# Where a Trainium2 kernel keeps and asks for its weights between a dense stage and a 64-step loop

## The chip, the core and the metric

The kernel runs on one core of one Trainium2 chip. The metric is the device time of one execution in microseconds (us), as the median of several runs. The core has five engines that work side by side: TensorE (PE) multiplies matrices, VectorE (DVE) and ScalarE (ACT) work on elements, GpSimd (POOL) does so too, and SyncE (SP) issues transfers. Transfers (DMA) can be issued from SP, ACT and POOL; each of the three has a queue of its own, which the profile calls q1 (SP), q10 (ACT) and q0 (POOL).

## The reference

Two independent parts are computed and laid side by side in the output.

```python
# part A: a gated long convolution over 2048 rows, 1024 columns
kv = shifted(k, shift_k) * v
y  = irfft(rfft(kv padded) * rfft(ssm_k padded)) + kv * ssm_D
a  = q * y

# part B: attention with a memory, segment after segment (32 rows each, 64 segments)
mem = mem0                                    # 8 rows
for s in range(64):
    h = concat([mem, x[32 rows of s]])        # 40 rows x 1024
    q, k, v = h @ Wq, h @ Wk, h @ Wv          # 32 heads of 128
    o = softmax(mask(q k^T * scale)) v
    o = o @ Wo
    mem = o[:8]                               # goes into the next segment
    out[s] = o[8:]
```

Wq, Wk, Wv and Wo have 1024 x 4096 bf16 values each, 8.4 MB, 33.6 MB together[...].

## The kernel before, in words

**Weights.** Each of the four matrices is cut into 16 chunks of 128 partitions x 2048 values, 512 KB (0.524 MB) each. A chunk is named (m, kc, g): m is 0 for K, 1 for Q, 2 for V, 3 for the output weights; kc is its block of rows; g is the first or second half of the heads. `order` lists the 64 chunks in the order in which a segment uses them. The 21 that `STREAM` picks are *streamed*: they are copied once to a tensor WS in device memory and from there loaded into a ring of six slots (`wring`, line 658, on SP's queue) in every segment. Two of them are kept on the chip from the second segment on, so the loop has 1218 ring loads. The other 43 are *resident*: they lie on the chip during the whole loop.

**Homes of the residents.** `parts[0]` (12 chunks of K and Q, tiles `Wmid`) are loaded before the dense stage. `parts[1]` (19 chunks, tiles `Wres`) are the 11 resident chunks of V and 8 more called `extra`: four of K first half and four of Q second half. The last 12, `late` (two of Q, ten of the output weights, tiles `Wlate`), are loaded once everything before the loop is over.

**Stages.** Part A comes first: stage 1 (0 to some 125 us), the spectra (to some 300 us) and the last stage (to some 358 us). Into the gaps of A's spectra and last stage, `fill()` puts *dense* slices: for 8 rows of each segment, K and Q of all heads are computed ahead (`dense`, line 550), one call for each of K first half, K second half, Q first half, Q second half. Each call ends with one store of 2 MB, `REC<-stage` (line 562), on SP's queue; it consists of 8192 pieces of 256 bytes. Chunks that have no home yet go through `pw`, a rotating pool of eight tiles that is closed with the pre-loop scope. `group` (line 515) issues the loads of the eight chunks of one (m, g), and for streamed ones the copy to WS on POOL's queue (line 526).

After A, V of the same rows is computed (line 598): 2 halves x 4 row blocks x 4 column blocks x 8 chunks, 256 matmuls; their results go to VBD in 32 stores (line 602). The weights of the second half are asked for with the second half's `group` call. After V's calls `extra` is loaded (line 609), then `late` (line 614, in turn on SP and ACT), then the loop begins: six `fetch` calls fill the ring (line 658), the records of the first segment are loaded (`rec`, line 707), and the memory rows (Y0, line 725, on ACT's queue); the first transposes on PE (line 713) need Y0 and make the memory part of hT, which every projection needs.

**What sets the order.** Outside the loop a scheduler orders the instructions of each engine; so V loads, VBD stores and loads of `extra` stand interleaved on SP. The loop is ordered by hand (`tc.manual_schedule()`). An engine issues its instructions in order, its DMAs too. The DMAs of SP and ACT share eight completion semaphores in rotation; before one is used again, its issuer waits until the DMA that had it last has landed. A tile that takes the place of an earlier one waits until the earlier one's readers are done.

Of the kernel before, what the change touches and what calls it, by code (L numbers as in the profile page):

```python
# [9 lines left out]
BF = mybir.dt.bfloat16  # L10
# [15 lines left out]
N2, N3 = 12, 19  # L26
# [358 lines left out]
def b_kernel(ctx: ExitStack, tc, x, mem0, Wq, Wk, Wv, Wo, outb, n_seg, run_a):  # L385
    nc = tc.nc
    SEG = 32
    NX = 24
# [18 lines left out]
    streamed = set()  # L407
    for i in STREAM:
        streamed.add(order[i])
    resident = [ch for ch in order if ch not in streamed]  # L410
    groups = [(m, g) for m in (0, 1, 2) for g in range(2)]
    own = {mg: [ch for ch in resident if ch[0] < 3 and (ch[0], ch[2]) == mg] for mg in groups}
    parts = [(own[0, 1] + own[1, 0])[:N2], own[2, 0] + own[2, 1]]
    extra = [ch for ch in own[0, 0] + own[1, 1] + resident if ch not in parts[0] + parts[1]][:N3 - len(parts[1])]
    parts[1] = parts[1] + list(dict.fromkeys(extra))
    late = [ch for ch in resident if ch not in parts[0] and ch not in parts[1]]


    ring_order = [ch for ch in order if ch in streamed]
# [1 line left out]
    def dram_chunk(ch):  # L421
        m, a, g = ch
        return Wo_v[a] if m == 3 else W_v[m][a, g]

    def dst_view(ap, ch):
        return ap.rearrange("p (hh d) -> p hh d", hh=2) if ch[0] == 3 else ap

    def stream_src(ch):
        return WS[ring_order.index(ch), :, 0:2048]
# [3 lines left out]
    REC = dram.tile([128, n_seg, 768], BF, name="REC")  # L433
    VBD = dram.tile([n_seg, 8, 4, 4, 256], BF, name="VBD")
    WS = dram.tile([len(ring_order), 128, PITCH], BF, name="WS")
    res = {}
# [10 lines left out]

    c0 = ExitStack()
    xtp = c0.enter_context(tc.tile_pool(name="b0_xt", bufs=1, side="right"))
    pring = c0.enter_context(tc.tile_pool(name="b0_ring", bufs=8, side="right"))  # L450
    st = c0.enter_context(tc.tile_pool(name="b0_st", bufs=2, side="right"))
    XBT = xtp.tile([128, 8, n_seg, 8], BF, name="XBT")

    def pw():
        return pring.tile([128, 2048], BF, tag="pw", name="pw")

    def slot16(shape, dt, name):
        return st.tile(shape, dt, tag="stage", name=name)
# [4 lines left out]
    def stage1_done():  # L463
        make_consts()
        pools["mid"] = ctx.enter_context(tc.tile_pool(name="b_wmid", bufs=1, reuse_waits="tile"))
        for i, ch in enumerate(parts[0]):
            res[ch] = pools["mid"].tile([128, 2048], BF, name=f"Wmid{i}")[:]
        make_xbt()
        for _ in dense(0, 0):
            pass  # L470
# [41 lines left out]
            nc.scalar.copy(XBT[:, :, 16 * tb:16 * tb + 16, :].rearrange("p k s t -> p k (s t)"),  # L512
                           tp[:].rearrange("p (k c) -> p k c", k=8))

    def group(m, g):
        ws = []
        for kc in range(8):
            ch = (m, kc, g)
            if ch in res:
                nc.sync.dma_start(res[ch], dram_chunk(ch))  # L520
                ws.append(res[ch])
            else:
                t = pw()
                nc.sync.dma_start(t[:], dram_chunk(ch))
                if ch in streamed:
                    nc.gpsimd.dma_start(stream_src(ch), t[:])
                ws.append(t[:])
        return ws

    def x_block(b):  # L530
        X_sb = st.tile([128, 1024], BF, tag="X_sb", name="X_sb")
        xq[b % 2].dma_start(X_sb[:], x[b * 128:(b + 1) * 128, :])
        tp = ps0.tile([128, 1024], BF, tag="ps0", name="xt_ps")
        for kc in range(8):
            nc.tensor.transpose(tp[:, kc * 128:(kc + 1) * 128], X_sb[:, kc * 128:(kc + 1) * 128], ident[:])
        xt = st.tile([128, 4, 8, SEG], BF, tag="xt", name="xt")
        nc.vector.tensor_copy(xt[:], tp[:].rearrange("p (k j t) -> p j k t", k=8, j=4))
        nc.gpsimd.dma_start(REC[:, 4 * b:4 * b + 4, 0:256], xt[:].rearrange("p s k t -> p s (k t)"))
# [3 lines left out]
    def evac(dst, src):  # L542
        flip[0] ^= 1
        if flip[0]:
            nc.scalar.copy(dst, src)
        else:
            nc.vector.tensor_copy(dst, src)


    def dense(m, g, ws=None):  # L550
        ws = ws or group(m, g)
        stage = st.tile([128, n_seg, 16, 8], BF, tag="stage", name="stage")
        for hl in range(16):
            ps = ps0.tile([128, 512], F32, tag="ps0", name="kb_ps")
            for kc in range(8):
                nc.tensor.matmul(ps[:], lhsT=ws[kc][:, hl * 128:(hl + 1) * 128],  # L556
                                 rhs=XBT[:, kc].rearrange("p s t -> p (s t)"),
                                 start=(kc == 0), stop=(kc == 7))
            evac(stage[:, :, hl, :], ps[:].rearrange("p (s t) -> p s t", t=8))
            yield  # L560
        o = 256 * (m + 1) + 128 * g
        nc.sync.dma_start(REC[:, :, o:o + 128], stage[:].rearrange("p s h t -> p s (h t)"))

    def slices():
        k1, q0 = group(0, 1), group(1, 0)
        n = 0
        for m, g, ws in ((0, 1, k1), (1, 0, q0), (1, 1, None)):
            for _ in dense(m, g, ws):
                n += 1
                if n % 3 == 0:  # L570
                    x_block(n // 3 - 1)
                yield

    rest = slices()

    def fill():
        next(rest, None)

    run_a(pw, slot16, stage1_done, fill)

    wres3 = ctx.enter_context(tc.tile_pool(name="b_wres", bufs=1, reuse_waits="tile"))
    for i, ch in enumerate(parts[1]):
        res[ch] = wres3.tile([128, 2048], BF, name=f"Wres{i}")[:]

    with c0, c0p:
        for _ in rest:
            pass
        for ch in ring_order:
            if ch[0] == 3:
                nc.gpsimd.dma_start(dst_view(stream_src(ch), ch), dram_chunk(ch))  # L590
        for g in range(2):
            ws = group(2, g)
            for tb in range(4):
                vst = st.tile([128, 4, 512], BF, tag="stage", name="vst")
                for c in range(4):
                    ps = ps0.tile([128, 512], F32, tag="ps0", name="vb_ps")
                    for kc in range(8):
                        nc.tensor.matmul(ps[:], lhsT=XBT[:, kc, 16 * tb:16 * tb + 16, :].rearrange("p s t -> p (s t)"),
                                         rhs=ws[kc][:, c * 512:(c + 1) * 512], start=(kc == 0), stop=(kc == 7))
                    evac(vst[:, c, :], ps[:])  # L600
                for c in range(4):
                    nc.sync.dma_start(
                        VBD[16 * tb:16 * tb + 16, :, c, :, g * 128:(g + 1) * 128].rearrange("s t i e -> (s t) i e"),
                        vst[:, c, :].rearrange("p (i e) -> p i e", i=4))


        for ch in parts[1]:
            if ch in extra:
                nc.sync.dma_start(dst_view(res[ch], ch), dram_chunk(ch))

    wl = ctx.enter_context(tc.tile_pool(name="b_wlate", bufs=1, side="right", reuse_waits="tile"))
    for i, ch in enumerate(late):
        res[ch] = wl.tile([128, 2048], BF, name=f"Wlate{i}")[:]
        (nc.sync if i % 2 == 0 else nc.scalar).dma_start(dst_view(res[ch], ch), dram_chunk(ch))
    ring = ctx.enter_context(tc.tile_pool(name="b_ring", bufs=1, side="right", reuse_waits="tile"))
    one = ctx.enter_context(tc.tile_pool(name="b_one", bufs=1, side="right", reuse_waits="tile"))
    two = ctx.enter_context(tc.tile_pool(name="b_two", bufs=2, side="right", reuse_waits="tile"))
# [100 lines left out]
    with tc.manual_schedule():  # L718
# [3 lines left out]
        Y0 = one.tile([128, 256], BF, tag="PT", name="Y0")  # L722
        nc.vector.memset(Y0[:], 0.0)
        for dq in range(4):
            nc.scalar.dma_start(Y0[32 * dq + NX:32 * dq + SEG, :], mem0[:, dq * 256:(dq + 1) * 256])
        nc.tensor.matmul(SB[:], lhsT=ident[:], rhs=QBm[:].rearrange("p c i w -> p (c i w)"), start=True, stop=True,
                         skip_group_check=True)

# [43 lines left out]
        for s in range(n_seg):  # L772
# [132 lines left out]
            q0 = Proj(1, 0).run(4)  # L905
# [3 lines left out]
            q0 = q0.run(4).evac()  # L909
            k1 = Proj(0, 1).run(4)  # L910
            QT0 = one.tile([128, 4, 4, 32], BF, tag="QT", name="QT")
            nc.vector.tensor_copy(QT0[:], transposes(q0))
            k1 = k1.run(4).evac()
            scores(0, QT0, KT0)
            softmax_a()
            q1 = Proj(1, 1).run(4)
# [4 lines left out]
            q1 = q1.run(4).evac()  # L921
# [18 lines left out]
            if last:  # L940
                own = Tail(OTB, b, ps_acc.tile([128, 512], F32, tag="acc", name="own_acc")[:, 0:256])
# [21 lines left out]
def kernel(  # L963
# [26 lines left out]
    with ExitStack() as ctx_b:  # L990
        b_kernel(ctx_b, tc, B_x[0], B_mem0[0],
                 B_Wq.rearrange("d h e -> d (h e)"), B_Wk.rearrange("d h e -> d (h e)"),
                 B_Wv.rearrange("d h e -> d (h e)"), B_Wo.rearrange("h e d -> (h e) d"),
                 outb, n_seg, run_a)
# [35 lines left out]
```

## Time and profile before

| what | value |
|---|---|
| median of 7 runs | 2194.92 us (2188.84 to 2202.79) |
| the profiled execution, its own time | 2193.48 us |
| its span in the profile | 2191.7 us |
| PE, DVE, ACT, POOL busy | 79%, 40%, 29%, 19% of the span |
| moved by DMA | 807.80 MB, mean 369 GB/s |
| first matmul of V, last matmul of V | 379.1 us, 442.9 us |
| first matmul of the loop's first projection | 464.6 us |

The page divides the span into 40 slices of 54.8 us; a digit is the busy share of a slice in tenths. A line of waits names the waiting engine and line, what it waited for, the total in us, how often, and the longest. A line of an engine's order in time has start and length in us; "SPq", "ACTq" are the DMA instructions of those engines' queues, and their length is what the issue took, not the transfer. In "us to landing" a DMA is counted from issue until its data are there.

### The profile page before, as it was taken

How to read it: one execution, taken by the hardware profiler on the slowest of the kernel's cores; microseconds unless marked ns; L12 is line 12 of the kernel's file. 1: busy time of each engine (PE TensorE's matmuls, PEld its weight loads, DVE VectorE, ACT ScalarE, POOL GpSimd, SP SyncE). 2: the span in 40 equal slices, each digit the busy share in tenths (PEclk: the TensorE clock that was granted, in tenths of full speed). 3: DMA queues.
4: the chain of work that ended last, by engine and by line, in shares of the span. 5: the costliest groups of instructions: out<-in, count | busy, mean ns of one | idle time of the engine just before them, and what ended most of it. 6: DMA issues, size and time to landing. Idle time of an engine off the chain costs nothing. (4 is left out here: it accounts for less than half of the span.)

```text
span 2191.7 us, 81529 instructions
## 1 busy us (share of the span) xinstructions
PE 1722.7 (79%) x35636; PEld 927.2 (42%) x35636; DVE 884.6 (40%) x2702; ACT 638.9 (29%) x1118; POOL 412.9 (19%) x1103
## 2 busy tenths in 40 slices
PE   4679975957888888888887888887878878887886
PEld 2233332424444444444444444444444444444444
DVE  8828853123333333333333333333333333333333
ACT  5845620112222222222222222222222222222222
POOL 5003421001111111111111111111111211111111
PEclk9889987979999999999999999999999999999999
DMA  9989989899999999999999999999999999999997
GB/s 322 349 294 364 306 259 319 256 358 398 383 375 391 381 375 388 394 372 392 394 393 378 394 394 393 391 395 389 392 393 377 394 392 383 390 391 382 387 394 272
DMA packets 294286, 807.80 MB, mean 369 GB/s; under 512 B 84940, under 2 KB 84972, under 8 KB 293927
## 3 DMA queue, kind: packets, MB, share of 16 engines
q1 hardware_dynamic: 263592, 738.36, 89.1%
q0 software_dynamic: 23536, 50.51, 6.9%
q10 hardware_dynamic: 6800, 13.72, 1.7%
q8 instruction: 279, 4.57, 0.9%
q14 instruction: 79, 0.65, 0.1%
HBM read 743.06 MB, written 62.39 MB: 368 GB/s over the span
## 5 line engine op out<-in xcount | busy, mean ns | idle before, releaser
L806 PEld LDWEIGHTS <-rec 128*32 128x32 bf16 x12351 | 324.1, 96 | 468.1 <-issue 248.7
L806 PE MATMUL acc<-wring,rec 128*32 128x512 bf16 (+1 forms) x3777 | 375.9, 386 | 132.6 <-DMA wring<-WS 116.9
L815 ACT CAST qkv_sb<-acc 128x512 bf16<-128x512 f32 x384 | 225.1, 586 | 674.0 <-PE acc L806 670.9
L806 PE MATMUL acc<-Wres,rec 128*32 128x512 bf16 x4864 | 394.4, 383 | 0.3 <-issue 0.3
L892 PEld LDWEIGHTS <-OT 128*32 128x32 bf16 x8192 | 216.8, 96 | 178.9 <-issue 152.5
L892 PE MATMUL yacc<-Wlate,OT 128*32 128x256 bf16 x5120 | 221.0, 273 | 14.8 <-issue 13.5
L892 PE MATMUL yacc<-wring,OT 128*32 128x256 bf16 x3072 | 154.6, 276 | 98.3 <-DMA wring<-WS 58.5
L806 PE MATMUL acc<-Wmid,rec 128*32 128x512 bf16 x3072 | 224.9, 382 | 0.0
L752 PEld LDWEIGHTS <-OTB 128*16 128x16 bf16 x4096 | 105.4, 90 | 104.4 <-issue 93.8
L878 ACT CAST OT<-OTp 128x512 bf16<-128x512 f32 x128 | 75.0, 586 | 242.2 <-PE OTp L870 239.1
L908 DVE COPY KT<-tps 128x512 bf16<-128x512 bf16 x64 | 27.2, 425 | 292.4 <-PE tps L821 292.4
L707 POOL DMA_DIRECT2D rec<-REC x64 | 37.4, 584 | 566.3 <-issue 269.8
L879 DVE CAST OTB<-OTp 128x128 bf16<-128x128 f32 x128 | 37.3, 292 | 262.6 <-ACT OT L878 262.6
L647 DVE TENSOR_SCALAR wring<-OTp 128x384 int32<-128x384 int32 x126 | 112.3, 891 | 55.9 <-PE acc L806 52.7
L752 PE MATMUL SB<-Wlate,OTB 128*16 128x256 bf16 x2480 | 100.9, 283 | 34.6 <-DVE SB L743 19.7
L782 POOL COPY KT<-rec 128x128 bf16<-128x128 bf16 x128 | 38.7, 302 | 436.0 <-PE SB L830 427.9
L836 DVE TENSOR_REDUCE mx<-SB 128x5 f32<-128x200 f32 x128 | 47.1, 368 | 179.5 <-PE SB L830 179.5
L767 POOL DMA_DIRECT2D out_dram<-YB x128 | 73.1, 577 | 238.8 <-DVE YB L765 215.5
L752 PE MATMUL SB<-wring,OTB 128*16 128x256 bf16 x1488 | 78.5, 273 | 37.0 <-DVE SB L731 29.8
L821 PE MATMUL tps<-ident,qkv_sb 128*128 128x128 bf16 x1024 | 101.0, 221 | 8.0 <-DVE wring L647 0.2
L821 PEld LDWEIGHTS <-qkv_sb 128*128 128x128 bf16 x1024 | 62.7, 97 | 104.9 <-ACT qkv_sb L815 67.1
L556 PE MATMUL kb_ps<-XBT,pw 128*128 128x512 bf16 x320 | 87.7, 397 | 9.9 <-ACT XBT L512 8.0
(214 smaller groups left out, 2304.8 us busy)
## 6 DMA issues: line engine op xcount, KB each, us to landing
wring<-WS SPq DMA_DIRECT2D x1218, 512.0 KB, 7.2
rec<-REC POOLq DMA_DIRECT2D x64, 192.0 KB, 5.9
SK<-s_sb SPq DMA_DIRECT2D x16, 512.0 KB, 4.4
SU<-s_sb SPq DMA_DIRECT2D x16, 512.0 KB, 4.3
Ug<-SU SPq DMA_DIRECT2D x32, 256.0 KB, 6.0
Kg<-SK ACTq DMA_DIRECT2D x32, 256.0 KB, 5.5
REC<-stage SPq DMA_DIRECT2D x4, 2048.0 KB, 15.4
SZ<-zs SPq DMA_DIRECT2D x31, 256.0 KB, 3.4
```

Of the source, the lines that this page charges most:

```text
L556: nc.tensor.matmul(ps[:], lhsT=ws[kc][:, hl * 128:(hl + 1) * 128], rhs=XBT[:, kc].rearrange("p s t -> p (s t)"), start=(kc == 0), stop=(kc ...
L647: nc.vector.tensor_scalar(out=dst, in0=src, scalar1=0, scalar2=None, op0=ALU.bitwise_or)
L707: nc.gpsimd.dma_start(rec[:], REC[:, s, :])
L752: nc.tensor.matmul(self.acc[32 * dq:32 * dq + W, x - o:y - o], lhsT=self.OTB[:, c, 4 * g + i, :], rhs=r, start=first and not self.seeded, ...
L767: nc.gpsimd.dma_start(bass.AP(outb.tensor, outb.offset + (SEG * NB * self.b + NX) * 2048 + 256 * dq, [[2048 * SEG, NB], [2048, 8], [1, 256 ...
L782: nc.gpsimd.tensor_copy(KT[:, :, :, 32:40], KBs[:, 128 * g:128 * g + 128].rearrange("p (c i t) -> p i c t", c=4, i=4))
L806: nc.tensor.matmul(self.acc[32 * c:32 * c + 32, x - 512 * c:y - 512 * c], lhsT=hT[:, kc, :], rhs=r, start=(kc == 0 and x == 512 * c), stop ...
L815: nc.scalar.copy(sb[:], self.acc[:])
L821: nc.tensor.transpose(tp[:, i * 128:(i + 1) * 128], sb[:, i * 128:(i + 1) * 128], ident[:])
L836: nc.vector.tensor_reduce(out=mx[:], in_=S, op=ALU.max, axis=AX.X)
L878: nc.scalar.copy(OT[:], o_view[:, :, :, 0:32])
L892: nc.tensor.matmul(yacc[32 * dq:32 * dq + 32, x - o:y - o], lhsT=OT[:, c, i, :], rhs=r, start=(h == 0 and x == o), stop=(h == 31), tile_po ...
```

## The change

It does five things. (1) Six of the eight Q second-half chunks, those that are resident (`kept_q1`), get the `pw` tiles in which the dense stage uses them as their home for the loop; `pw` becomes eight tiles with fixed tags in a pool that stays open, and the loads of the eight chunks are asked for at the start of Q first half (six) and of Q second half (two). `extra` then holds the four K chunks and four output chunks, and `late` six output chunks, of which two take the remaining `pw` tiles. (2) All 16 V loads are issued ahead of V's first matmul: the five streamed ones go into three tiles of later `extra` chunks and into two `pw` tiles. (3) `extra` is loaded on POOL's queue: five chunks ahead of V compute, three when V is done with their tiles. (4) `late` is issued on ACT's queue alone, so that the ring loads follow the VBD stores on SP directly; Y0 is loaded on POOL's queue. (5) The four REC stores move from SP's to ACT's queue.

```diff
--- before.py
+++ after.py
@@ -411,9 +411,11 @@
     groups = [(m, g) for m in (0, 1, 2) for g in range(2)]
     own = {mg: [ch for ch in resident if ch[0] < 3 and (ch[0], ch[2]) == mg] for mg in groups}
     parts = [(own[0, 1] + own[1, 0])[:N2], own[2, 0] + own[2, 1]]
-    extra = [ch for ch in own[0, 0] + own[1, 1] + resident if ch not in parts[0] + parts[1]][:N3 - len(parts[1])]
-    parts[1] = parts[1] + list(dict.fromkeys(extra))
-    late = [ch for ch in resident if ch not in parts[0] and ch not in parts[1]]
+    kept_q1 = own[1, 1][:6]
+    placed = parts[0] + parts[1] + kept_q1
+    extra = [ch for ch in own[0, 0] + own[1, 1] + resident if ch not in placed]
+    extra = list(dict.fromkeys(extra))[:N3 - len(parts[1])]
+    late = [ch for ch in resident if ch not in placed and ch not in extra]
 
 
     ring_order = [ch for ch in order if ch in streamed]
@@ -447,12 +449,17 @@
 
     c0 = ExitStack()
     xtp = c0.enter_context(tc.tile_pool(name="b0_xt", bufs=1, side="right"))
-    pring = c0.enter_context(tc.tile_pool(name="b0_ring", bufs=8, side="right"))
+    pring = ctx.enter_context(tc.tile_pool(name="b0_ring", bufs=1, reuse_waits="tile"))
     st = c0.enter_context(tc.tile_pool(name="b0_st", bufs=2, side="right"))
     XBT = xtp.tile([128, 8, n_seg, 8], BF, name="XBT")
 
-    def pw():
-        return pring.tile([128, 2048], BF, tag="pw", name="pw")
+    pw_next = [0]
+
+    def pw(k=None):
+        if k is None:
+            k = pw_next[0] % 8
+            pw_next[0] += 1
+        return pring.tile([128, 2048], BF, tag=f"pw{k}", name="pw")
 
     def slot16(shape, dt, name):
         return st.tile(shape, dt, tag="stage", name=name)
@@ -512,19 +519,19 @@
             nc.scalar.copy(XBT[:, :, 16 * tb:16 * tb + 16, :].rearrange("p k s t -> p k (s t)"),
                            tp[:].rearrange("p (k c) -> p k c", k=8))
 
-    def group(m, g):
-        ws = []
-        for kc in range(8):
+    def group(m, g, temps={}, which=range(8), ws=None):
+        ws = ws or [None] * 8
+        for kc in which:
             ch = (m, kc, g)
             if ch in res:
                 nc.sync.dma_start(res[ch], dram_chunk(ch))
-                ws.append(res[ch])
+                ws[kc] = res[ch]
             else:
-                t = pw()
+                t = temps[ch]() if ch in temps else pw()
                 nc.sync.dma_start(t[:], dram_chunk(ch))
                 if ch in streamed:
                     nc.gpsimd.dma_start(stream_src(ch), t[:])
-                ws.append(t[:])
+                ws[kc] = t[:]
         return ws
 
     def x_block(b):
@@ -559,12 +566,21 @@
             evac(stage[:, :, hl, :], ps[:].rearrange("p (s t) -> p s t", t=8))
             yield
         o = 256 * (m + 1) + 128 * g
-        nc.sync.dma_start(REC[:, :, o:o + 128], stage[:].rearrange("p s h t -> p s (h t)"))
+        nc.scalar.dma_start(REC[:, :, o:o + 128], stage[:].rearrange("p s h t -> p s (h t)"))
 
     def slices():
         k1, q0 = group(0, 1), group(1, 0)
+        q1 = [None] * 8
+        first = [kc for kc in range(8) if (1, kc, 1) in kept_q1]
+        rest = [kc for kc in range(8) if kc not in first]
         n = 0
-        for m, g, ws in ((0, 1, k1), (1, 0, q0), (1, 1, None)):
+        for m, g, ws in ((0, 1, k1), (1, 0, q0), (1, 1, q1)):
+            if (m, g) == (1, 0):
+                for ch, k in zip(kept_q1, (4, 5, 6, 7, 0, 1)):
+                    res[ch] = pw(k)[:]
+                group(1, 1, which=first, ws=q1)
+            if (m, g) == (1, 1):
+                group(1, 1, {(1, kc, 1): (lambda k=k: pw(k)) for kc, k in zip(rest, (2, 3))}, rest, q1)
             for _ in dense(m, g, ws):
                 n += 1
                 if n % 3 == 0:
@@ -580,7 +596,13 @@
 
     wres3 = ctx.enter_context(tc.tile_pool(name="b_wres", bufs=1, reuse_waits="tile"))
     for i, ch in enumerate(parts[1]):
-        res[ch] = wres3.tile([128, 2048], BF, name=f"Wres{i}")[:]
+        res[ch] = wres3.tile([128, 2048], BF, tag=f"Wres{i}", name="Wres")[:]
+
+    def more(i):
+        return wres3.tile([128, 2048], BF, tag=f"Wmore{i}", name="Wmore")
+
+    v_temp = [(2, kc, g) for g in range(2) for kc in range(8) if (2, kc, g) in streamed]
+    homes_v = [lambda i=i: more(i) for i in range(len(v_temp) - 2)] + [lambda k=k: pw(k) for k in (2, 3)]
 
     with c0, c0p:
         for _ in rest:
@@ -588,8 +610,14 @@
         for ch in ring_order:
             if ch[0] == 3:
                 nc.gpsimd.dma_start(dst_view(stream_src(ch), ch), dram_chunk(ch))
+        temps = dict(zip(v_temp, homes_v))
+        wv = [group(2, g, temps) for g in range(2)]
+        for i, ch in enumerate(extra):
+            if i >= len(v_temp) - 2:
+                res[ch] = more(i)[:]
+                nc.gpsimd.dma_start(dst_view(res[ch], ch), dram_chunk(ch))
         for g in range(2):
-            ws = group(2, g)
+            ws = wv[g]
             for tb in range(4):
                 vst = st.tile([128, 4, 512], BF, tag="stage", name="vst")
                 for c in range(4):
@@ -603,15 +631,16 @@
                         VBD[16 * tb:16 * tb + 16, :, c, :, g * 128:(g + 1) * 128].rearrange("s t i e -> (s t) i e"),
                         vst[:, c, :].rearrange("p (i e) -> p i e", i=4))
 
-
-        for ch in parts[1]:
-            if ch in extra:
-                nc.sync.dma_start(dst_view(res[ch], ch), dram_chunk(ch))
+        for i, ch in enumerate(extra):
+            if i < len(v_temp) - 2:
+                res[ch] = more(i)[:]
+                nc.gpsimd.dma_start(dst_view(res[ch], ch), dram_chunk(ch))
 
     wl = ctx.enter_context(tc.tile_pool(name="b_wlate", bufs=1, side="right", reuse_waits="tile"))
     for i, ch in enumerate(late):
-        res[ch] = wl.tile([128, 2048], BF, name=f"Wlate{i}")[:]
-        (nc.sync if i % 2 == 0 else nc.scalar).dma_start(dst_view(res[ch], ch), dram_chunk(ch))
+        t = pw(2 + i) if i < 2 else wl.tile([128, 2048], BF, name=f"Wlate{i}")
+        res[ch] = t[:]
+        nc.scalar.dma_start(dst_view(res[ch], ch), dram_chunk(ch))
     ring = ctx.enter_context(tc.tile_pool(name="b_ring", bufs=1, side="right", reuse_waits="tile"))
     one = ctx.enter_context(tc.tile_pool(name="b_one", bufs=1, side="right", reuse_waits="tile"))
     two = ctx.enter_context(tc.tile_pool(name="b_two", bufs=2, side="right", reuse_waits="tile"))
@@ -722,7 +751,7 @@
         Y0 = one.tile([128, 256], BF, tag="PT", name="Y0")
         nc.vector.memset(Y0[:], 0.0)
         for dq in range(4):
-            nc.scalar.dma_start(Y0[32 * dq + NX:32 * dq + SEG, :], mem0[:, dq * 256:(dq + 1) * 256])
+            nc.gpsimd.dma_start(Y0[32 * dq + NX:32 * dq + SEG, :], mem0[:, dq * 256:(dq + 1) * 256])
         nc.tensor.matmul(SB[:], lhsT=ident[:], rhs=QBm[:].rearrange("p c i w -> p (c i w)"), start=True, stop=True,
                          skip_group_check=True)
 
```

## The prediction

> **What bounds the kernel now.** I read three lines of the page first: the slices, the DMA queues and the DMA issues.
>
> ```profile
> PE   4679975957888888888887888887878878887886
> DMA  9989989899999999999999999999999999999997
> GB/s 322 349 294 364 306 259 319 256 358 398 383 375 391 381 375 388 394 372 392 394 393 378 394 394 393 391 395 389 392 393 377 394 392 383 390 391 382 387 394 272
> ...
> q1 hardware_dynamic: 263592, 738.36, 89.1%
> ...
> wring<-WS SPq DMA_DIRECT2D x1218, 512.0 KB, 7.2
> REC<-stage SPq DMA_DIRECT2D x4, 2048.0 KB, 15.4
> ```
>
> A slice is 54.8 us. From the ninth on the core moves 375 to 395 GB/s with its DMA engines over 90% busy, and q1, SP's queue, carries 738 of the 808 MB. That is the loop: 1218 ring loads of 512 KB, bound by transfers. In the first eight slices, 0 to about 460 us, the rate is 256 to 364 GB/s: there something other than bytes is late. The waits of PE between 300 and 520 us name it:
>
> ```profile
> PE vb_ps L598 <- DMA Wres<-in_B_Wv_dram: 24.5, 5, 20.2
> PE tps L713 <- DMA Y<-in_B_mem_dram: 13.2, 1, 13.2
> PE y_ps L375 <- DMA zt<-SZ: 10.2, 5, 4.7
> ```
>
> (Columns: total us, times, longest.) V's weights cost 24.5 us, one wait of 20.2; the memory rows Y hold the loop's first transposes for 13.2. Why were the weights late? SP's own queue in order of time (start, duration):
>
> ```profile
> 355.29 0.34 SPq L524 DMA_DIRECT2D pw<-in_B_Wv_dram  x1
> 356.33 0.33 SPq L381 DMA_DIRECT2D out_dram<-ot  x1
> 357.56 0.56 SPq L562 DMA_DIRECT2D REC<-stage  x1
> 359.37 10.77 SPq L381 DMA_DIRECT2D out_dram<-ot  x1
> ```
>
> The small output store behind the 2 MB REC store took 10.77 us to issue, so SP gets free 12.6 us after the REC store went out, and the next V load stands at 370.73. The same happens behind the stores at 160.97 (next DMA 13.59 us) and 225.60 (10.80 us). The three stages, read from the windows:
>
> ```profile
> 360.00:370.00 10.00, 0.00 (x0) 0.00 (x0) 0.47 (x1) 0.00 (x0) 0.56 (x1) 0.59 1.08 261
> ...
> 430.00:440.00 10.00, 10.00 (x48) 4.52 (x47) 1.68 (x3) 1.76 (x3) 0.00 (x0) 1.00 0.42 86
> 440.00:450.00 10.00, 3.06 (x15) 1.18 (x12) 1.81 (x5) 0.59 (x1) 0.00 (x0) 0.86 0.83 258
> 450.00:460.00 10.00, 0.61 (x1) 0.10 (x1) 0.77 (x4) 0.00 (x0) 1.99 (x7) 0.50 1.04 378
> ```
>
> After the stretch and its length the first column is PE's busy time, the last two are DMA share and GB/s. PE stands from 358.9 to 379.1; then it computes V without a break from 389.8 (last first-half weight at 388.7) to 442.9; then it stands again until 464.6, while the DMA engines load what is still missing.
>
> **What the Trainium skill says.** "DMA: Bandwidth & Descriptors", section "Issuing engines are not separate DMA queues": DMAs from several engines run on the same 16 DMA engines and interleave; another issuer only saves sequencer time. The trace agrees on the engines: while the REC store ran at 360 to 370 their share stood at 1.08 with only 261 GB/s moved. But the sequencer time here is 12 us, not small. The same page, "Queues, rings and completion order": each DMA engine takes turns between queue rows packet by packet. The trace fits: beside the REC store at 225.6, key gathers on ACT's queue took 6.7 us to land, against 5.5 over all. So a REC store on ACT's queue lets SP's loads pass, but each slows the other.
>
> **The change part by part.** Six of the eight Q second-half chunks stay where the dense stage put them; they were loaded again later (4 as Wres, 2 as Wlate). Removed: 6 x 0.524 = 3.15 MB, at the loop's 390 GB/s 8.1 us of DMA time. Where it lay decides its worth. The four Wres reloads went out between 406 and 426 under V compute, with PE full: nothing saved directly, but their places are refilled by four output chunks that stood in the late list. So the late list after V falls from 12 to 6 chunks, 3.15 MB, and that is on the path.
>
> *Spectra stage (140 to 300 us).* The REC stores move to ACT's queue. SP no longer stops for some 12 us twice; PE idled about 3 us in each of the stretches 180 to 200 and 240 to 260, and part of it may come back. Against this, the next key gather on ACT stands eight to ten operations behind each store. ACT runs these in 8 to 10 us (13 casts in 10.2 us at 225 to 235), the queue is free after 12.3, so ACT stops for 2 to 5 us twice, with spectrum casts queued behind and PE waiting for those. Four Q loads also go out earlier, beside the first store. Gain and loss cancel: I take 0, bounds -5 to +6.
>
> *Last stage of A (300 to 358).* The last SZ store issued at 296.20 took 3.96 us behind a REC store; the first zt load needs it. That goes; the second zt load now waits for the REC store to land, as it did before. I take -2, bounds -4 to +1.
>
> *V start.* In the built program's order all 16 V loads follow A's last output store (about 361 us). Two go out earlier, but they are second-half chunks. SP issues four first-half chunks by 364. The fifth, (2,4,0), then waits on the completion semaphore that it shares with the last REC store: eight such semaphores go round over the DMAs of SP and ACT. The REC store alone needs some 9.5 us of DMA time (2.1 MB at the 218 GB/s seen beside it); sharing with four V chunks, two early ones, copies to WS and POOL's output chunks it lands about 377 to 380 instead of 372. Then 2.5 us of issue and 7.5 to 8.2 of landing (the Wres row) give 387 to 390, less the 2 us of the part above; before, 388.7. So the 11 us stall is mostly replaced by another wait: I take -2, bounds -10 (REC lands early) to +5. V compute, 256 matmuls at 0.216 us = 55.3, is unchanged.
>
> *Between V and loop.* Late loads sit on ACT alone, the ring is first on SP, Y rows on POOL. The Y wait goes, and so does SP's queue of late loads ahead of the ring (first ring load 457.8, 15 us after V). Late next: the third ring load shares a semaphore with the first late load, which lands 9.3 us after issue, so it goes out about 11 us after V, lands at 18; before, its like landed at about 24. The byte count agrees. From 440 to the first Y at 492.6 the engines moved 19.2 MB; 3.15 less and 0.5 more (one extra chunk that waits for V's end) are 16.6 MB, at 390 GB/s 42.5 us after V instead of 49.7. I take -6, bounds -10 to -2.
>
> *Loop.* Instruction order is the same on PE, DVE, ACT and POOL, and the ring still carries 1218 loads: 0. That cover is the DMA rate itself. If residents moved in SBUF changed it, 1% would be 17 us; nothing in the trace suggests it.
>
> Sum: 0 - 2 - 2 - 6 = **-10 us**. The profiled execution took 2193.48 (span 2191.7); it becomes 2183.5. The median of the seven runs lies 1.4 above it, so I predict 2185 for the median.
>
> **Rivals.**
> 1. *REC out of the way (large gain).* If REC lands within 15 us even when shared, V's first half is complete about 377, 11 earlier; with 2, 8 from the tail and 3 from the spectra stage, -24: 2171. For it: gathers beside a REC store were slowed by only 1.2 us. Against: those were 256 KB pieces, here some 5 MB compete.
> 2. *Tail hidden anyway (no change).* If A's stage and V start lose what the tail wins, say +3, 0, +2 and -5, the result is 2195. For it: the fifth V load's semaphore, and the third ring load's.
> 3. *ACT pays for SP (slower).* The REC store on ACT blocks the casts in the spectra stage: Kg gathers come after the queue is free and are late for their set too, 6 us at each of the two stores, and REC lands after 385, so that V starts 6 later: +12 +6 - 6 = +12: 2207. It decides once ACT's stop behind a store is over about 6 us, that is, if it reaches the gather in under 6 us. For it: PE was over 95% busy in much of this stage, so a stop counts in full. Against: eight casts took 8 us and more.
>
> **How the numbers follow.** A measurement of this kernel can tell about 0.3%, 6.6 us, from no change. Likeliest case (2178 to 2191) 0.50, rival 1 0.22, rival 2 0.18, rival 3 0.10. Below 2188.3 lie 0.44 of the likeliest case and all of rival 1: faster 0.66. The other 0.06 of the likeliest case and 0.16 of rival 2 make same 0.22; slower 0.12 is rival 3 and the upper 0.02 of rival 2. The range, 2168 to 2198, leaves out rival 3 and the lower end of rival 1, some 0.08: about 2 in 10.
>
> **What would show it.** In the changed profile: SP issues without the 10 us store behind REC; ACT's DMA issues show a 2 to 5 us one behind REC at about 173 and 237; V's first-half loads come in two parcels, four near 361 and four after 377; V compute ends near 439; the wait of tps on Y is gone and the loop's first matmul comes about 10 us after V, followed by a ring wait. HBM reads fall by 3.1 MB. Wrong would be: V ending before 430 (rival 1) or after 446 (rival 3), or loop windows of 100 us whose rate differs from 391 GB/s by over 1%.

## The result, and the profile after

The changed kernel is slower: 2215.84 us, median of 14 runs (2207.10 to 2222.17), against 2196.80 for the kernel before beside it (35 runs). The ratio is 1.0079, interval 1.0062 to 1.0097. The forecast was 2185. The profiled execution took 2214.37 us, its span is 2212.4.

The page of the kernel after, the lines that answer to those shown of before:

```profile
PE   4677986667778887888788888887887877888886
DMA  9978879879999999999999999999999999999996
GB/s 324 354 285 290 273 250 342 268 239 388 389 381 383 389 388 390 392 388 386 391 394 391 395 387 395 391 390 387 396 391 372 393 377 377 390 390 391 391 391 268
...
q1 hardware_dynamic: 228104, 722.63, 85.5%
...
HBM read 739.92 MB, written 62.39 MB: 363 GB/s over the span
...
REC<-stage ACTq DMA_DIRECT2D x4, 2048.0 KB, 25.0
```

From the tenth slice on the rate is what it was, 372 to 396 GB/s but for the last slice (before: 372 to 398): the loop did not change. The loss lies in the first nine slices, which moved 239 to 354 GB/s; the fourth went from 364 to 290 and the ninth from 358 to 239. HBM read fell from 743.06 to 739.92 MB, the 3.1 MB that the kept Q chunks should save. Queue q1 carries 723 MB instead of 738. And a REC store now takes 25.0 us to land, as the page's median, where it took 15.4.

To place the loss I read five starts of matmuls from the trace and use them for every kernel below: the last of the spectra (z_ps), the last of A (y_ps), the first and last of V (vb_ps), and the first of the loop's first projection.

| us | spectra end | A end | V first to last | loop starts | V end - A end | loop start - V end | span - loop start |
|---|---|---|---|---|---|---|---|
| before | 295.2 | 358.6 | 379.1 to 442.7 | 464.6 | 84.1 | 21.9 | 1727.1 |
| after | 319.6 | 377.0 | 389.8 to 468.9 | 488.2 | 91.9 | 19.3 | 1724.2 |

So the spectra stage lost 24.4 us, of which A's last stage gave 6.0 back; V's stage lost 7.8; the step from V to the loop won 2.6, the loop 2.9. The sum is +20.7, the difference of the spans.

**Spectra.** ACT's own order in time, 155 to 260 us, in the kernel after (start, duration):

```profile
161.59 0.59 ACTq L569 DMA_DIRECT2D REC<-stage  x1
171.35 13.71 ACTq L276 DMA_DIRECT2D Kg<-SK  x1
...
239.29 0.54 ACTq L569 DMA_DIRECT2D REC<-stage  x1
249.46 5.47 ACTq L276 DMA_DIRECT2D Kg<-SK  x1
```

The first key gather behind each of these two REC stores took 13.71 and 5.47 us to issue. ACT's casts stood behind it; PE waits, 100 to 380 us:

```profile
PE Ure_ps L306 <- ACT Kre L318: 15.1, 2, 12.1
```

PE was busy for 39.7 us of the three stretches 160 to 180, 180 to 200 and 240 to 260 taken together; in the kernel before it was busy for 53.7 of the same 60. The first of the three, before and after (PE's busy time follows the length):

```profile
160.00:180.00 20.00, 19.58 (x118) 7.13 (x118) 17.27 (x30) 12.29 (x24) 7.60 (x8) 1.00 1.05 310
```

```profile
160.00:180.00 20.00, 12.73 (x73) 4.69 (x72) 11.02 (x18) 5.18 (x10) 6.37 (x8) 0.90 1.04 360
```

SP, which the move was meant to free, stood too. Its waits, 160 to 300 us, in the kernel after:

```profile
SPq L527 <- DMA REC<-stage: 17.9, 1, 17.9
```

Five Q loads went out between 160.2 and 168.7 us; the sixth waited until the store had landed and stands at 186.68. The two have no data in common; what ties them is a shared completion semaphore, the route that the forecast describes for V's fifth load.

**V.** SP's order in time and its longest wait, 355 to 480 us, in the kernel after:

```profile
381.54 2.52 SPq L527 DMA_DIRECT2D Wres<-in_B_Wv_dram  x2
406.36 0.33 SPq L531 DMA_DIRECT2D Wmore<-in_B_Wv_dram  x1
```

```profile
SPq L531 <- DMA REC<-stage: 22.2, 1, 22.2
```

Two parcels of V loads, as forecast, and the load between them waits for the REC store's semaphore; but for 22.2 us, since the store, issued at 375.99, took 30.3 us to land. The windows show PE with little to do meanwhile (3.87 us of ten), and then with nothing, at 202 GB/s:

```profile
390.00:400.00 10.00, 3.87 (x8) 0.91 (x7) 0.00 (x0) 0.00 (x0) 1.28 (x2) 0.50 1.03 395
400.00:410.00 10.00, 0.00 (x0) 0.00 (x0) 0.00 (x0) 0.00 (x0) 0.00 (x0) 0.50 0.83 202
```

**Between V and loop.** PE's waits, 320 to 540 us:

```profile
PE vb_ps L626 <- DMA Wres<-in_B_Wv_dram: 17.0, 6, 12.4
PE vb_ps L626 <- DMA Wmore<-in_B_Wv_dram: 13.6, 2, 12.0
...
PE SB L755 <- DVE QBm L731: 9.9, 1, 9.9
PE tps L742 <- DMA Y<-in_B_mem_dram: 7.7, 1, 7.7
```

The wait on Y is down from 13.2 to 7.7, but not gone. Beside it stands one of 9.9 on QBm, a tile that DVE clears before the loop. That one is not new; PE's waits, 300 to 520 us, in the kernel before have it too:

```profile
PE SB L726 <- DVE QBm L702: 7.1, 1, 7.1
```

So the two waits together fell from 20.3 to 17.6 us, about the 2.6 that this step won.

### The profile page after: what moved, and what is told of

Its sections match the earlier page's. It is cut to its first block, busy times and chain, and to the rows that moved or that the text cites. A ratio compares the mean times of both kernels' runs of the same rounds, so it can differ in the third digit from the quotient of the medians.

```text
span 2212.4 us, 81510 instructions
## 1 busy us (share of the span) xinstructions
PE 1727.0 (78%) x35636; PEld 925.7 (42%) x35636; DVE 884.0 (40%) x2702; ACT 637.9 (29%) x1118; POOL 419.6 (19%) x1115
## 3 DMA queue, kind: packets, MB, share of 16 engines
HBM read 739.92 MB, written 62.39 MB: 363 GB/s over the span
## 5 line engine op out<-in xcount | busy, mean ns | idle before, releaser
L835 PE MATMUL acc<-Wres,rec 128*32 128x512 bf16 x2816 | 221.2, 380 | 0.0
L835 PE MATMUL acc<-pw,rec 128*32 128x512 bf16 x1536 | 130.4, 382 | 0.0
L921 PE MATMUL yacc<-Wlate,OT 128*32 128x256 bf16 x2048 | 99.1, 274 | 12.0 <-issue 11.7
L921 PE MATMUL yacc<-Wmore,OT 128*32 128x256 bf16 x2048 | 104.5, 273 | 2.1 <-issue 1.3
```

What stands on the lines that cost most here:

```text
L835: nc.tensor.matmul(self.acc[32 * c:32 * c + 32, x - 512 * c:y - 512 * c], lhsT=hT[:, kc, :], rhs=r, start=(kc == 0 and x == 512 * c), stop ...
L921: nc.tensor.matmul(yacc[32 * dq:32 * dq + 32, x - o:y - o], lhsT=OT[:, c, i, :], rhs=r, start=(h == 0 and x == o), stop=(h == 31), tile_po ...
```

## The experiments

All are timed against the kernel before, run beside them on the same chip. Places of the profiled executions, columns as above:

| us | spectra end | A end | V first to last | loop starts | V end - A end | loop start - V end |
|---|---|---|---|---|---|---|
| e1_rec_sp | 296.8 | 362.7 | 385.2 to 454.6 | 473.5 | 91.9 | 18.9 |
| e2_before_rec_act | 322.3 | 375.8 | 392.1 to 464.1 | 486.3 | 88.3 | 22.2 |
| e3_last_rec_sp | 320.2 | 377.2 | 400.0 to 471.0 | 489.9 | 93.8 | 18.9 |
| e4_first_recs_sp | 299.5 | 363.9 | 376.8 to 455.4 | 474.5 | 91.5 | 19.1 |
| e5_last_rec_behind_v | 298.3 | 362.2 | 372.7 to 454.9 | 473.9 | 92.7 | 19.0 |
| e6_extra_behind_v | 296.7 | 359.7 | 378.9 to 448.5 | 467.4 | 88.8 | 18.9 |
| e7_one_ahead_of_late | 298.9 | 363.0 | 386.1 to 456.3 | 471.1 | 93.3 | 14.8 |
| e8_three_together | 296.2 | 360.8 | 370.7 to 452.9 | 467.4 | 92.1 | 14.5 |
| e9_own_v_buffers | 296.0 | 364.4 | 374.9 to 441.5 | 456.1 | 77.1 | 14.6 |
| e10_rec_on_act_in_v | 293.0 | 357.3 | 367.0 to 437.7 | 452.5 | 80.4 | 14.8 |
| e11_before_rec_in_v | 295.6 | 356.0 | 371.6 to 434.9 | 457.2 | 78.9 | 22.3 |

The loop took 1722.8 to 1738.0 us in these single executions, with no pattern by kernel. I therefore read causes from the places up to the loop, and the time from the medians.

### The REC stores: e1 to e4

e1, the change with its REC stores back on SP:

```diff
-        nc.scalar.dma_start(REC[:, :, o:o + 128], stage[:].rearrange("p s h t -> p s (h t)"))
+        nc.sync.dma_start(REC[:, :, o:o + 128], stage[:].rearrange("p s h t -> p s (h t)"))
```

> The changed kernel with all four REC stores back on SP's queue. Theory 1 (the REC stores on ACT's queue stop ACT behind themselves and, through the shared semaphores, SP): A's last matmul returns from 377 to about 359 us, V's first half is complete about 30 us after it as in the kernel before, V ends near 443, the 2.8 us in front of the loop and the 2.8 us in the loop that the change won stay: 0.3% faster than the kernel before, ratio 0.997. Theory 2 (the loads asked for earlier compete with the REC stores for the DMA engines, whoever issues them): the four early Q loads stretch the first REC store to 25 us here too, A ends at 370 or later, ratio 1.005 or more.

Measured: 2197.97 us, ratio 1.0020 (1.0005 to 1.0035). Neither theory's ratio came: A ends at 362.7, so the early Q loads alone do not delay it as theory 2 had it (the first store lands after 16.9 us), but V ends at 454.6 and not near 443.

e2, the kernel before with that one line turned the other way:

```diff
-        nc.sync.dma_start(REC[:, :, o:o + 128], stage[:].rearrange("p s h t -> p s (h t)"))
+        nc.scalar.dma_start(REC[:, :, o:o + 128], stage[:].rearrange("p s h t -> p s (h t)"))
```

> The kernel before with only the four REC stores moved to ACT's queue. Theory 1: the loss is here without anything else of the change: ACT's gather behind the first REC store takes 5 to 14 us to issue, A ends 10 to 18 us later, ratio 1.005 to 1.010. Theory 2: without the early Q and V loads a REC store lands within 17 us on ACT's queue as well, SP gains its free time, A ends no later than 360 us, ratio 0.993 to 1.000.

Measured: 2215.54 us, ratio 1.0096 (1.0068 to 1.0125). As theory 1 had it, one line is enough for the whole loss. The rest of the change, e1, wins nothing: it is 0.2% slower, and its interval just leaves out no change. ACT's order in time in e2 shows the same stop:

```profile
162.43 0.59 ACTq L562 DMA_DIRECT2D REC<-stage  x1
172.30 13.84 ACTq L276 DMA_DIRECT2D Kg<-SK  x1
```

How long such a stop lasts is told by when the store lands. The DMA parts of 155 to 190 us in the kernel before and of 160 to 190 in the one after, in this order:

```profile
REC<-stage SPq DMA_DIRECT2D x1, 2048.0 KB, 16.8
```

```profile
REC<-stage ACTq DMA_DIRECT2D x1, 2048.0 KB, 25.0
```

In e2 it is 25.4. In the kernel after the gather's issue ended at 185.06, 23.5 us behind the store; at the second store (landing 17.9 us) it ended 15.6 us behind it. In before, on SP, the next DMA is a Q load; SP's order in time:

```profile
161.58 13.59 SPq L524 DMA_DIRECT2D pw<-in_B_Wq_dram  x1
```

Its issue ended 14.2 us behind the first store. These ends are 1.5 to 2.6 us short of the store's landing (up to 4.3 short at other stores of before and e1): what follows a store on its queue waits nearly until it is done. On ACT the first store is done later. The reading that fits is that SP, which stood still behind it before, now issues loads beside it: five Q chunks went out around the store in e2 and in after before SP, too, had to wait for it (19.0 us in e2), while in before the first came out behind the stop. Two readings support this: on SP's queue, with V's last loads and POOL's in flight, the last store also takes 25.0 us (e9), and on ACT's, with fewer loads beside it, the second took 17.9. No run holds SP's loads back with the store on ACT, so it stays a reading. The early Q loads of the change aren't needed for it: e2 does not have them.

e3 and e4 divide the stores:

```diff
 e3, of the change:
-        nc.scalar.dma_start(REC...)
+        (nc.sync if (m, g) == (1, 1) else nc.scalar).dma_start(REC...)
 e4, of the change:
-        nc.scalar.dma_start(REC...)
+        (nc.scalar if (m, g) == (1, 1) else nc.sync).dma_start(REC...)
```

> The changed kernel with only the last REC store (Q second half, ahead of V) back on SP. Theory 1: the spectra loss stays (A ends near 377 us), the wait of the fifth V load of 22 us on the REC store's semaphore goes, V's first half is complete about 30 us after A instead of 37.5: 8 us better than the changed kernel, ratio 1.004. Theory 2: V's loads are late by competition in any case; no better than the changed kernel, ratio 1.008.

Measured: 2219.76 us, ratio 1.0111 (1.0085 to 1.0137).

> The changed kernel with the first three REC stores back on SP, the last on ACT. Theory 1: A ends near 359 us (18 us better than the changed kernel), V's first half still 37 us after it, ratio 1.000. Theory 2: the early Q loads still delay A, A ends at 370 or later, ratio 1.005.

Measured: 2198.87 us, ratio 1.0010 (0.9996 to 1.0025). The first three stores on ACT's queue cost some 13 us at A's end (377.0 and 377.2 with them there, 362.7 and 363.9 without). My theory on the fourth failed: I held ACT's queue, through the semaphore, to be what made V late, and putting the store back on SP made V no earlier. SP's order in time in e3 shows the stop that took the semaphore's place:

```profile
376.14 0.57 SPq L569 DMA_DIRECT2D REC<-stage  x1
378.10 14.71 SPq L381 DMA_DIRECT2D out_dram<-ot  x2
392.91 0.39 SPq L531 DMA_DIRECT2D pw<-in_B_Wv_dram  x1
```

On SP the V loads stand behind the store on the queue (14.7 us), on ACT behind its semaphore (22.2 us, but four chunks ahead of it). V end - A end is 93.8 and 91.9. On either queue the store is in the way.

### What else V and the loop wait for: e5 to e8

These start from e1. e5 puts the last REC store behind the sixteenth V load on SP; e6 puts the five early loads of `extra` on POOL behind the copy of chunk (2,0,1) to WS; e7 opens the pool `one`, which holds QBm and Y, ahead of the pool of `late`; e8 is the three together.

```diff
 e5:
+        with tc.issue_after(<the last V load on SP>):
+            <the store of (1, 1)>
 e6:
+        with tc.issue_after(<WS copy of (2, 0, 1)>):
             for i, ch in enumerate(extra):
                 if i >= len(v_temp) - 2:
                     ...
 e7:
+    one = ctx.enter_context(tc.tile_pool(name="b_one", bufs=1, side="right", reuse_waits="tile"))
     wl = ctx.enter_context(tc.tile_pool(name="b_wlate", bufs=1, side="right", reuse_waits="tile"))
     ...
-    one = ctx.enter_context(tc.tile_pool(name="b_one", bufs=1, side="right", reuse_waits="tile"))
```

> The kernel of e1 (all REC stores on SP), with the last REC store tied behind the sixteenth V load on SP. Theory 1 (what comes ahead of V's first-half loads on a queue, or holds their semaphore, sets V's start): V's first half is complete 15 to 20 us after A's last matmul instead of 37, V ends about 18 us earlier relative to A, less up to 6 us if the first VBD stores have to stand behind the REC store; ratio to the kernel before 0.995. Theory 2 (V's first half waits for the sum of bytes asked for at that time, POOL's output chunks among them, in any order): still 30 us or more after A; ratio 1.000 or more.

Measured: 2198.79 us, ratio 1.0016 (1.0002 to 1.0029). V starts at 372.7 instead of 385.2 (e1) and still ends at 454.9. One of PE's waits, 320 to 520 us, in e5:

```profile
PE vb_ps L635 <- ACT vst L554: 9.1, 2, 8.8
```

The wait on Wres fell from 28.0 (e1) to 17.8, and this wait on V's casts, 0.3 in e1, took its place.

> The kernel of e1, with the five early extra loads on POOL tied behind the WS copy of chunk (2,0,1), which can only go when V's first half has landed. Theory 1: SP stays blocked behind the last REC store, V's first half is complete 32 to 36 us after A; ratio 1.001. Theory 2: the 2.6 MB taken out of the competition are worth 7 us, V's first half is complete about 30 us after A as in the kernel before; ratio 0.999.

Measured: 2195.40 us, ratio 1.0001 (0.9982 to 1.0020). V end - A end falls by 3.1 us against e1, with the wait on Wres at 21.8. That fits POOL's loads competing with V's, but it is one pair of executions (e7, the same as e1 in this stage, is 1.4 from it). The ratio's interval overlaps that of e1.

> The kernel of e1, with the pool of the loop's small tiles (record, QBm, Y0) opened ahead of the late weights' pool, so that these tiles take the place of XBT and not of the last V results. Theory of the tail: between V and the loop the memsets, the record and Y0 wait until the last VBD stores have landed (9.7 us on PE) and only then are loaded (7.6 us); with the wait gone the stretch from V's last to the loop's first matmul falls from 19 to about 11 us; ratio 0.998. Rival: the ring and late loads set that stretch (DMA rate 370 GB/s), it stays at 17 us or more; ratio 1.002.

Measured: 2196.97 us, ratio 1.0009 (0.9992 to 1.0026). The wait on QBm falls from 9.7 to 1.6, so it came from the place that `one` took over (in before DVE waits 5.5 us of it on a VBD store; in e1 the trace names no reader). The loop starts 14.8 us after V instead of 18.9; the rest is a wait for ring loads, 9.0 in acc instead of 1.7. In the median I can't tell it from nothing.

> The three edits of e5, e6 and e7 together. Theory 1 and the theory of the tail: V's first half complete 14 us after A, V's end about 68 to 74 us after A (before 84), stretch to the loop 11 us: 16 to 20 us better than the kernel before, less 4 us of a later end of A: ratio 0.993. Theory 2: V's end 80 us after A or later, ratio 0.998.

Measured: 2195.54 us, ratio 1.0002 (0.9988 to 1.0017). V starts at 370.7 and again ends late. In e8 the waits of PE (320 to 520 us) and of ACT (365 to 420 us) have these lines:

```profile
PE vb_ps L636 <- ACT vst L554: 14.7, 2, 14.4
```

```profile
ACT vst L554 <- DMA REC<-stage: 18.3, 1, 18.3
```

ACT's cast of V waits for the REC store to land, and DVE's does so for 16.5 us. Either because V's results take over the `stage` buffer from which the store reads (the pool has two under that name, `vst` included), or because the VBD stores stand behind REC on SP.

### Buffer or queue: e9, e10, e11

e9 is e8 with other buffers for half of V's results; e10 also moves the last REC store into V on ACT's queue; e11 does these two things to the kernel before, and nothing else.

```diff
 e9:
-                vst = st.tile([128, 4, 512], BF, tag="stage", name="vst")
+                if tb < 2:
+                    vst = <two tiles [128, 2, 512] with the tags "X_sb" and "xt">
+                else:
+                    vst = <as before>
 e10 and e11 also:
                     evac(vst[c], ps[:])
+                if held:
+                    with tc.issue_after(<ACT's second cast of V>):
+                        <the store of (1, 1), on ACT's queue>
```

> e8_three_together, with other buffers for V's results in row blocks 0 and 1 of each half: two tiles of 128 x 1024 in the places of X_sb and xt, which are free by then, in place of the `stage` buffers, one of which holds the last REC store's data until it has landed. Theory 'the buffer': in e8 the casts vst waited for REC's landing (18.3 us on ACT) because they needed its buffer; now the first two row blocks don't, the PE wait on vst falls from 14.7 to under 3 us, V ends 10 to 12 us earlier than 453, the first loop matmul comes near 457, and the time is 0.994 to 0.996 of before. Theory 'the queue': the VBD stores behind REC on SP hold V; then the wait on vst only moves two row blocks later and the time stays at 1.000.

Measured: 2181.48 us (2175.60 to 2188.02), ratio 0.9930 (0.9906 to 0.9954). In e9 PE's waits (320 to 520 us), SP's order in time (355 to 480 us) and the DMA part of 365 to 400 us show:

```profile
PE vb_ps L641 <- ACT vst L554: 0.2, 1, 0.2
```

```profile
384.96 0.56 SPq L572 DMA_DIRECT2D REC<-stage  x1
387.62 55.38 SPq L645 DMA_DIRECT2D VBD<-vst  x32
```

```profile
REC<-stage SPq DMA_DIRECT2D x1, 2048.0 KB, 25.0
```

The store stands on SP as in e8, ahead of all 32 VBD stores, and lands no sooner: 25.0 us. The first VBD store behind it still takes 20.3 us to issue (19.8 in e8). But the first casts no longer need its buffer: ACT's wait on it falls from 18.3 to 3.8, PE's on vst from 14.7 to 0.2, and V ends 11.4 us earlier (441.5). PE's wait for V's weights is the same (13.5 and 13.4 on Wres). e9 also gives V's results more buffers, but in e8 no cast waited for a VBD store, so it isn't their number. The buffer was the cause.

> e9_own_v_buffers, with the last REC store on ACT's queue behind the second cast of V that ACT does, so that neither a V load nor a VBD store stands behind it on a queue; the sixth VBD store shares its completion semaphore. Theory 'the buffer': V as in e9 within 3 us, first loop matmul near 455, time 0.993 to 0.996 of before. Theory 'the queue': only here the wait on vst goes, and this one is 8 us or more faster than e9.

Measured: 2182.08 us (2181.29 to 2184.76), ratio 0.9938 (0.9921 to 0.9955): as e9. V end - A end is 80.4 against 77.1. The queue of the VBD stores makes no difference to the time. Both kernels beat the one before and the changed one; e9 and e10 can't be told apart.

> The kernel before, with only its last REC store moved onto ACT's queue behind the second cast of V that ACT does, and the buffers of V's results as in e9. Nothing else of the change. If the REC store ahead of V was what cost the kernel before its late V start: SP's V loads follow A's last output store without the stop of 10.8 us, V computes without a break from some 10 us earlier than 389.8 and ends near 433 instead of 442.7. Half or more of it should arrive at the loop: first loop matmul 455 to 459 (before 464.6), time 0.995 to 0.998 of before. If what comes after V is bound by bytes alone, the loop starts as before, near 464, and the time is 1.000.

Measured: 2193.40 us, ratio 0.9990 (0.9975 to 1.0005). The places came as expected: V ends at 434.9, the loop starts at 457.2, 7.4 us earlier than before. The medians say 1.8 us, with up to 5.5 inside the interval, less than I expected. Its profiled execution, 2185.09 us, is among the shorter of its 22 runs (2183.74 to 2204.97), so the one trace may overstate it. That the store alone is worth moving in the kernel before is not shown.

## Why the prediction was wrong

**The bound, and the bytes: right.** The loop runs at its old rate, and 3.1 MB less are read. The slices were read a little off: eight of them end at 438 us, not 460, and the ninth still moved 358 GB/s.

**Spectra, 0 (bounds -5 to +6): wrong, +24.4.** This is the step that failed. It foresaw ACT's stop, its place and the casts behind it, and sized it by "the queue is free after 12.3" and "2 to 5 us twice". The 12.3 is too short for the first store even on SP: the 13.59 that the text gives there makes 14.2. With that and ACT at the gather after 9.8 us the stop would still have been 4.4, inside the forecast. It was 13.71, because the store landed after 25.0 instead of 16.8 us: the time had been read on SP, where the stop itself kept SP's loads back. The second, 5.47, was just above the forecast. The text had said in its second place from the Trainium skill that "each slows the other", and applied it to V's start, not here. "SP no longer stops" was wrong as well: at the first store SP waited 17.9 us, by the semaphore route that the text saw only at V's start. PE's waits name ACT's casts, not SP's loads, so ACT's stop is what PE felt. The rise in the spectra is 5.2 us more than ACT's two stops together (19.2); where these 5.2 come from is open.

**Rival 3 named the direction, not the route.** It said 6 us at each store, if ACT reached the gather in under 6 us. ACT reached it after 9.8 and 10.2 us, as the main case had it; the stop was long because the store took longer. Its size, 2207, was too small as well. Its sign, V ending after 446, came: V ended at 468.9.

**Last stage of A, -2 (-4 to +1): measured -6.0.** From spectra end to A end the three kernels with the first stores on ACT (after, e2, e3) took 53.5 to 57.4 us, the others 60.4 to 68.4. So it comes with the stores on ACT. The stop of the last SZ store is gone as forecast (0.32 us instead of 3.96); what the rest is, no run separates.

**V start, -2 (-10 to +5): the mechanism right, the size off.** The semaphore and the two parcels came as written. REC was to land "about 377 to 380", some 20 us after its old place at 357.56, by way of "9.5 us of DMA time" and sharing; it took 30.3, and SP's wait was 22.2 us. V end - A end grew by 7.8, outside the bounds. The -2 had also taken V's compute as unbroken: it was not, PE stood from 400 to 410. PE's waits for V's weights came to 30.6 us, before 24.5. Undoing the queue alone doesn't mend it (e1 and e3: 91.9 and 93.8), and the queue alone costs 4.2 (e2: 88.3): with the store on SP, the rest of the change loses the 7.8 too. POOL's loads of `extra`, which the forecast had counted as bytes beside REC, are 3.1 of it by e6; the remainder is open. The buffer behind the store is no part of the miss, since PE waited only 0.2 us for V's casts here. It was the next limit, hidden until e5 and e8 let V start sooner, and then worth 11.4 us (e8 to e9).

**Between V and loop, -6 (-10 to -2): measured -2.6.** "The Y wait goes" was wrong: it fell by 5.5. And the wait on QBm was missing from the sum. It had stood in the waits of before with 7.1 us and grew to 9.9. e7 takes it down to 1.6, and the gap falls to 14.8, that is 7.1 below before, about the size of the forecast. The bytes were counted rightly; a tile's place was not looked at.

**Loop, 0:** measured -2.9 in one pair of executions, inside what single executions differ by.

Sum: forecast -10, measured +20.7 in the spans. +24.4 instead of 0 in the spectra makes most of the difference of 30.7; -4.0, +9.8, +3.4 and -2.9 are the other four.

On the Trainium skill: "DMA: Bandwidth & Descriptors", section "Issuing engines are not separate DMA queues", holds the sequencer time of starting a DMA to be usually small beside the DMA. For these stores the measurement differs: the DMA behind one took 5.5 to 13.8 us to issue on ACT (4.0 to 13.6 on SP in the kernel before), and on ACT that is compute time. The part of that section that says all queues run on the same 16 engines agrees with the 16.8 against 25.0 us, as far as the later landing is competition.

## What to carry to other kernels

A long store that other work stands behind is not freed by another queue: ask what the new queue's engine has to do next, and reckon its landing with the transfers that the move sets free, not with the time it had when it blocked them. Then follow its buffer and its completion semaphore as well as its queue: its semaphore stopped SP in the spectra and ahead of V, and the gain came only with its buffer (e8 to e9: 14 us by a change of buffers alone, each timed beside the kernel before on its own chip). Which of the earlier edits e9 needs, no run tests. An edit that removes a wait is worth what the next wait leaves of it, so it may look worthless alone (e5: 1.0016) and pay in company (e9, which contains it: 0.9930).

## What the runs showed of the hardware

The stop behind a store of 8192 pieces of 256 bytes followed the store's landing, not its issue: it ended 14.2, 15.6 and 23.5 us after the store was issued, where it landed after 16.8, 17.9 and 25.0. The same 2 MB landed in 14.1 to 19.1 us on SP's queue (before and e1) and in 17.9 to 30.3 us on ACT's, beside SP's loads (after). On SP too it took 24.7 and 25.0 us where other loads were in flight (e8, e9).
